# An attention + two-MoE kernel: the first duo transposed in two-token blocks, identity transposes ahead of it, and steps of the first expert's set-up moved

## The chip, the core and the metric

The kernel runs on one core of a Trainium2 chip. The metric is the device time of one execution, in microseconds. Before the change it was 596.75 us (median of three runs, 595.57 to 597.35).

## What is computed

Sigmoid attention, then two mixture-of-experts layers, all in fp32; `x` is the attention's output, a row per token with its 12 heads side by side.

```python
scores = scale * q @ k^T - log(S)            # 4 batches, 12 heads, S = 448, head_dim = 64
attn   = sigmoid(scores) @ v
# first MoE: rows with x @ w_skip > 0 only
e      = argmax(x @ w_gate)                  # 8 experts
y      = gate * (relu(x @ w1[e]) @ w2[e])    # 768 -> 1024 -> 768
x      = x + y
# second MoE: all rows
e      = argmax(normed(x) @ normed(emb)^T / tau)
out    = gate * (relu(x @ v1[e]) @ v2[e])
```

## The kernel before

The program is written out in order: each engine (PE is TensorE, ACT ScalarE, DVE VectorE, POOL GpSimd, SP the queue that issues most loads) works its own instructions strictly in that order and waits on semaphores.

**Attention** goes over 12 duos `w`, each four heads of a batch: `i` and `j` number the two pairs. A duo has 7 steps `h` of 64 keys. The loop counts `g = 7w + h`. In a step PE makes the scores of `h` (`score`, L596, four matmuls side by side into one of two `psS` tiles), ACT turns them into `A` by a sigmoid (L600), and two steps later PE multiplies `A` with `v` (`av`, L614) into two `psO` tiles. `take_x` (L523 on ACT, L525 on DVE) copies a finished duo's `psO` into `xT`. Loads of `k` and `q` of later duos are issued from SP (L553), of `v` from ACT (L565); from the second duo on, DVE transposes `k` and `q` in SBUF (`turn`, L587).

**The first duo** is loaded otherwise (L542): four consecutive tokens lie in one of 112 partitions, `(p c)` with `c` of 4. `turn_first` (L569) is called for k and q of `i = 0`, then of `i = 1`. For each `j` PE makes four transposes, one token of 64 values at a time (L575), and one copy takes the 64 x 448 result to `kT` or `qT`: DVE's for `j = 0` (L583), ACT's for `j = 1` (L581).

**Beside the attention** stand small steps, one list entry per `g`. When three batches are done (`b == B - 2`, at `g = 64`), a table `at` (L661) gives the steps for the first dense expert: `s1` to `s3` route batch 2; `gates` (L326) makes two sigmoids on ACT, then five DVE instructions; `plan_first` (L352) chooses a batch and expert on DVE; `start` reads the choice into registers and issues four weight loads of 768 KB on SP; `gate_cols` (L681) builds a diagonal matrix of the gates on DVE (L686); `rows` (L689) multiplies it with ones on PE (L692) and copies it back on ACT (L693); then seven calls of `split_gated` (L700), each a DVE product (L703), an ACT copy to the high part `xs` (L705) and a DVE subtraction for the low part (L706) of the chunk before.

**After the attention**, `split_unit` cuts weights into high and low parts (ACT L764, DVE L765) and `dense` (L774 to L776) makes three matmuls for each product.

Of the kernel before, what the change touches and what calls it, by code (L numbers as in the profile page):

```python
# [10 lines left out]
F32 = mybir.dt.float32  # L11
F32R = mybir.dt.float32r
I32 = mybir.dt.int32
AF = mybir.ActivationFunctionType
ALU = mybir.AluOpType
# [6 lines left out]
def sigmoid_attention_moe_moe_kernel(  # L22
# [15 lines left out]
    nc = tc.nc  # L38
# [287 lines left out]
    def gates(R, b0, b1):  # L326

        n = (b1 - b0) * C
        e = sm.tile([P, 2, (B - 1) * C, NE], F32, tag="ge", name="ge", bufs=1)
        s = sm.tile([P, B * C], F32, tag="gs", name="gs", bufs=1)  # L330
        sh = (R.SH[:, b0:b1] if R.m == 0 else R.SH).rearrange("p b c e -> p (b c) e")
        nc.scalar.activation(e[:, 0, :n], sh, AF.Sigmoid)
        nc.scalar.activation(e[:, 1, :n], sh, AF.Sigmoid, scale=-1.0)
        nc.vector.reciprocal(e[:, 1, :n], e[:, 1, :n])
        nc.vector.tensor_mul(e[:, 0, :n], e[:, 0, :n], e[:, 1, :n])
        nc.vector.reduce_sum(s[:, :n], e[:, 0, :n], axis=AX.X)
        nc.vector.tensor_single_scalar(s[:, :n], s[:, :n], 1e-9, op=ALU.add)
        nc.vector.reciprocal(K["gr"][R.m][:, b0:b1, :, 0], s[:, :n].rearrange("p (b c) -> p b c", c=C))

    def dense_gate(R, b, g=None):  # L340
        t = sm.tile([P, C, NE], F32, tag="dgt", name="dgt")
# [10 lines left out]
    def plan_first(R):  # L352

        n = B - 1
        t = sm.tile([128, 3, B], F32, tag="pl1", name="pl1", bufs=1)
        r = sm.tile([128, 4], F32, tag="pl1r", name="pl1r", bufs=1)
        fl = R.Fl[:, :n, 2]
        nc.vector.tensor_mul(t[:, 0, :n], fl, K["desc"][:, :n])
        nc.vector.reduce_max(r[:, 3:4], t[:, 0, :n], axis=AX.X)
        nc.vector.scalar_tensor_tensor(t[:, 1, :n], t[:, 0, :n], r[:, 3:4], fl, op0=ALU.is_equal, op1=ALU.mult)  # L360
        nc.vector.tensor_sub(K["rest"][:, :n], fl, t[:, 1, :n])
        nc.vector.tensor_single_scalar(r[:, 0:1], r[:, 3:4], 0.0, op=ALU.is_gt)
        nc.vector.tensor_mul(t[:, 2, :n], t[:, 1, :n], K["io"][:, :n])
        nc.vector.reduce_sum(r[:, 1:2], t[:, 2, :n], axis=AX.X)
        nc.vector.tensor_mul(t[:, 2, :n], t[:, 1, :n], R.Fl[:, :n, 3])
        nc.vector.reduce_sum(r[:, 2:3], t[:, 2, :n], axis=AX.X)
        nc.vector.tensor_copy(K["pa"][:, 0:3], r[:, 0:3])
# [159 lines left out]
    def attention():  # L527


        with ExitStack() as a:  # L530
# [27 lines left out]
            def load_v(w, *parts):  # L558
                b, d = duos[w]
                if "v" not in LDU[w]:  # L560
                    LDU[w]["v"] = ld.tile([128, 2, NH, D], F32, tag="v", name="v")
                t = LDU[w]["v"]
                for n in parts:
                    i, j = divmod(n, 2)
                    nc.scalar.dma_start(  # L565
                        t[KT * i : KT * i + KT, j], v[b, 4 * d + i + 2 * j].rearrange("(h r) d -> r h d", r=KT)
                    )

            def turn_first(nm, i):  # L569
                if i == 0:  # L570
                    ST[0, nm] = wk.tile([128, 2, S], F32, tag=nm + "T", name=nm + "T")
                ps = psS.tile([128, 2, 512], F32, tag="psS", name="ps_t")
                for j in range(2):
                    for c in range(C):
                        nc.tensor.transpose(  # L575
                            ps[:D, j, c * P : (c + 1) * P], LDU[0][nm][:, i, j, c * D : (c + 1) * D], ident[:P, :P]
                        )
                    src = ps[:D, j, :S].rearrange("r (c p) -> r p c", c=C)
                    dst = ST[0, nm][D * j : D * j + D, i].rearrange("r (p c) -> r p c", c=C)
                    if j:  # L580
                        nc.scalar.activation(dst, src, AF.Copy)  # L581
                    else:
                        nc.vector.tensor_copy(dst, src)  # L583

            def turn(w, nm):
                dst = ST[w, nm] = wk.tile([128, 2, S], F32, tag=nm + "T", name=nm + "T")
# [39 lines left out]
            nc.scalar.activation(bias, bias, AF.Sigmoid)  # L626
            nc.vector.memset(bias, -math.log(S))
            load_v(0, 0, 1, 2, 3)
            for i in range(2):
                turn_first("k", i)  # L630
                turn_first("q", i)
# [4 lines left out]
            for g in range(G + LAG):  # L636
                w, h = divmod(g, NH)
                if 0 < w < N - 2 and h == 0:
                    load_qk(w + 2)
                if g < G:  # L640
                    score(w, h)
                if w + 1 < N and 0 <= h - LAG < 4:
                    load_v(w + 1, h - LAG)
                if w + 1 < N and h in (3, 4):
                    turn(w + 1, "kq"[h - 3])
                for r in {LAG: (), LAG + 1: (LAG + 1, LAG)}.get(h, (LAG,)):
                    if g >= r:
                        av(*divmod(g - r, NH))
                for f in [todo.pop(0)] if todo and g >= 2 else late.get(g, ()):
                    if f:  # L650
                        f()
                done = g - LAG + 1
                if done % NH == 0 and done > 0:
                    b, d = duos[done // NH - 1]
                    if d == NP // 2 - 1 and b < B - 1:
                        assert not todo
                        s1, s2, s3 = route_stages(R1, b, x_of(b))
                        todo = [None, s1, s2, None, s3]
                        if b == B - 2:
                            fs = [s1, s2, s3, lambda: gates(R1, 0, B - 1), lambda: plan_first(R1)] + first_steps()  # L660
                            at = [g + i for i in (2, 3, 5, 8, 8, 10, 11, 12, 12, 13, 15, 16, 17, 18)] + [G]  # L661
                            todo, late = [], schedule({}, fs, at)
            return ST[N - 1, "o"]

# [45 lines left out]
    def first_steps():  # L710

        box = {}

        def start():
            pa = K["pa"]
            b = FIRST["b"] = nc.values_load(pa[0:1, 1:2], engines=XENG, min_val=0, max_val=B - 1)
            FIRST["e"] = nc.values_load(pa[0:1, 2:3], engines=[ENG.SP], min_val=0, max_val=NE - 1)
            load_unit(w1, w2, FIRST["e"], 0)
            load_unit(w1, w2, FIRST["e"], 1)
            box["p"] = split_gated(XST[0], b)  # L720

# [362 lines left out]
    def route2_steps(j, xs):  # L1084

        box = {}

        def halves(p):
            def f():
                if p == 0:  # L1090
                    box["b"] = batch_of(j)
                    box["p"] = split_batch(xs, box["b"])
                for g in box["p"][p : p + 2]:
                    g()

            return f

        return (
            [halves(p) for p in range(0, ND, 2)]
            + [lambda: raw(batch_of(j)), squares, squares_sum]  # L1100
            + route_stages(R2, j, lambda c: XR[:, c])
            + [scaled_logits, lambda: gates(R2, j, j + 1)]
        )


# [167 lines left out]
    nb_load = lambda: nc.values_load(K["pb"][0:1, 12:13], min_val=0, max_val=B - 1)  # L1273
    with tc.If(na > 0) as cmp:
        b, e = FIRST["b"], FIRST["e"]
        early = {0: s1, 2: s2, 4: s3, 5: [pl[0], lambda: gates(R1, B - 1, B)], 6: pl[1], 7: pl[2]}
        dense(XST[0], beside(units1(e), early), 0, NF // 2)
        NB["n"] = nb_load()
        with tc.If(NB["n"] > 0) as cmp2:
            steps = merge(next_dense(0), item_steps(R1, (10, 12, 15)), {12: lambda: raw(batch_of(0)), 15: squares})  # L1280
            dense(XST[0], beside(units1(e), steps), NF // 2)
            add_y(b)
            squares_sum()
            block1(1)
        with cmp2.Else():
            steps = merge(rest2(), item_steps(R1, (9, 11, 12)))
            dense(XST[0], beside(units1(e), steps), NF // 2)
            add_y(b)
            leftovers_now(lambda: start2(True))
            rare()  # L1290
    with cmp.Else():
        run({0: s1, 1: s2, 2: s3, 3: lambda: gates(R1, B - 1, B), 4: pl[0], 5: pl[1], 6: pl[2]})
        run(item_steps(R1, (0, 1, 2)))
        run(rest2())
        with tc.If(nb_load() > 0):
            run(next_dense(0))
            b, e = rest_regs(0)
            dense(XST[1], beside(units1(e), {}))
            add_y(b)
        leftovers_now(lambda: start2(True))  # L1300
        rare()
# [147 lines left out]
```

## Time and profile before

| | |
|---|---|
| median of the runs | 596.75 us |
| the profiled execution | 596.82 us |
| its span, first to last instruction | 595.0 us |
| PE busy | 572.8 us, 96% |
| DVE busy | 304.4 us, 51% |
| ACT busy | 275.2 us, 46% |
| fp32 score and value matmuls (L596, L614) | 88.2 and 86.4 us |

A line of the timeline gives start, duration, engine, line, operation, output and input tiles, the count of merged instructions, and in brackets the idle time before it and what ended that. `ACTq` and `SPq` are the issuing of DMAs by these engines. Each fp32 matmul of L596 and L614 is two records, each transpose one.

### The profile page before, as it was taken

The page shows a single profiled execution, that of the slowest core. Times are in us where ns is not written, and L with a number is a line of the kernel's source. Part 1 is how long each engine was busy: PE and PEld are TensorE (multiplying, and loading weights), DVE is VectorE, ACT ScalarE, POOL GpSimd, SP SyncE. Part 2 cuts the span into 40 slices and gives each one's busy share as a digit, 9 for nine tenths or more (in the row PEclk, how much of TensorE's full clock was granted, in tenths as well). Part 3 has the DMA queues.
Part 4 walks back from the last instruction along what each step waited for, and adds up shares of the span by engine and source line. Part 5 has one row for each costly group of instructions (what it writes and reads, how often), then busy time and mean ns, then how long its engine had stood idle before and what let it go on. Part 6 is the DMA issues. An engine that isn't in the chain of part 4 may idle for free. (4 is left out here: it accounts for less than half of the span.)

```text
span 595.0 us, 9925 instructions
## 1 busy us (share of the span) xinstructions
PE 572.8 (96%) x3722; PEld 440.0 (74%) x3722; DVE 304.4 (51%) x766; ACT 275.2 (46%) x447; POOL 7.5 (1%) x15
## 2 busy tenths in 40 slices
PE   5999999998999999999999999999999999999993
PEld 3365544534489897987868899979997999898881
DVE  2262435236757778562259664487347663542121
ACT  2676676666932374332138322752256322543020
POOL 2010000000000000000000000000000000000000
PEclk9999999999999999999999999999999999999997
DMA  9978877893460605234545060532317060642433
GB/s 150 117 118 132 109 120 109 122 119 87 166 204 6 209 4 165 103 107 159 188 158 190 2 211 1 188 118 80 133 58 248 1 214 0 223 159 83 159 108 100
DMA packets 139862, 73.31 MB, mean 123 GB/s; under 512 B 103858, under 2 KB 129798, under 8 KB 139792
## 3 DMA queue, kind: packets, MB, share of 16 engines
q1 hardware_dynamic: 116384, 65.94, 41.8%
q10 hardware_dynamic: 23216, 6.43, 6.0%
q8 instruction: 37, 0.61, 0.5%
q14 instruction: 33, 0.27, 0.1%
q0 software_dynamic: 192, 0.07, 0.1%
HBM read 66.90 MB, written 5.70 MB: 122 GB/s over the span
## 5 line engine op out<-in xcount | busy, mean ns | idle before, releaser
L774 PE MATMUL bank<-xs,h 128*128 128x448 f32 x288 | 107.6, 374 | 2.0 <-DVE xT L1165 0.9
L774 PE MATMUL y<-hh,h 128*128 128x448 f32 x288 | 108.5, 377 | 0.0
L794 ACT ACTIVATE hh<-bank 128x448 fp32r<-128x448 f32 x48 | 26.1, 543 | 177.4 <-PE bank L776 166.8
L775 PE MATMUL y<-hl,h 128*128 128x448 f32 x288 | 105.6, 367 | 0.0
L776 PE MATMUL y<-hh,l 128*128 128x448 f32 x288 | 105.6, 367 | 0.0
L776 PE MATMUL bank<-xs,l 128*128 128x448 f32 x288 | 105.3, 365 | 0.3 <-DVE l L765 0.3
L775 PE MATMUL bank<-xs,h 128*128 128x448 f32 x288 | 105.4, 366 | 0.0
L600 ACT ACTIVATE A<-psS,bias 128x896 f32<-128x896 f32 x84 | 83.4, 1006 | 35.9 <-PE psS L596 33.1
L596 PE MATMUL psS<-qT,kT 64*64 64x448 f32 x672 | 88.2, 554 | 0.0
L765 DVE TENSOR_TENSOR l<-r,h 128x512 fp32r<-128x512 f32 (+1 forms) x115 | 85.4, 792 | 4.8 <-ACT h L764 3.0
L795 DVE SCALAR_TENSOR_TENSOR hl<-bank,hh 128x448 fp32r<-128x448 f32 x48 | 29.9, 623 | 113.2 <-ACT hh L794 112.1
L614 PE MATMUL psO<-A,v 64*64 64x448 f32 x672 | 86.4, 539 | 0.0
L764 ACT ACTIVATE h<-r 128x512 fp32r<-128x512 f32 (+1 forms) x115 | 74.6, 710 | 0.0
L774 PEld LDWEIGHTS bank<-xs,h 128*128 128x128 f32 x288 | 54.0, 187 | 11.4 <-DVE hl L795 2.9
L774 PEld LDWEIGHTS y<-hh,h 128*128 128x128 f32 x288 | 54.1, 188 | 8.2 <-issue 2.9
L614 PEld LDWEIGHTS psO<-A,v 64*64 64x64 f32 x672 | 34.8, 133 | 32.3 <-issue 20.2
L776 PEld LDWEIGHTS bank<-xs,l 128*128 128x128 f32 x288 | 54.0, 188 | 5.5 <-DVE l L765 0.6
L776 PEld LDWEIGHTS y<-hh,l 128*128 128x128 f32 x288 | 54.1, 188 | 5.0
L775 PEld LDWEIGHTS y<-hl,h 128*128 128x128 f32 x288 | 54.2, 188 | 4.6 <-issue 0.2
L775 PEld LDWEIGHTS bank<-xs,h 128*128 128x128 f32 x288 | 54.1, 188 | 4.3
L596 PEld LDWEIGHTS psS<-qT,kT 64*64 64x64 f32 x672 | 32.8, 135 | 31.7 <-issue 17.4
L525 DVE COPY xT<-psO 64x448 f32<-64x448 f32 x24 | 14.9, 621 | 48.0 <-PE psO L614 47.7
(251 smaller groups left out, 452.8 us busy)
## 6 DMA issues: line engine op xcount, KB each, us to landing
r<-in_moe_w_dram SPq DMA_DIRECT2D x62, 768.0 KB, 5.9
v<-in_v_dram ACTq DMA_DIRECT2D x48, 112.0 KB, 3.6
k<-in_k_dram SPq DMA_DIRECT2D x44, 112.0 KB, 3.6
q<-in_q_dram SPq DMA_DIRECT2D x44, 112.0 KB, 4.0
out_dram<-row SPq DMA_DIRECT2D x3, 1344.0 KB, 6.9
out_dram<-row SPq DMA_DIRECT2D x1, 896.0 KB, 5.5
stg<-in_moe_w_dram SPq DMA_DIRECT2D x1, 768.0 KB, 6.4
row<-in_moe_w_dram SPq DMA_DIRECT2D x1, 768.0 KB, 8.2
```

Of the source, the lines that this page charges most:

```text
L525: nc.vector.tensor_copy(x, ps[64 * j : 64 * j + 64, :S])
L596: nc.tensor.matmul(ps[KT * i : KT * i + KT, j, :S], lhsT=kT[r, i, h * KT : (h + 1) * KT], rhs=qT[r, i], start=True, stop=True,)
L600: nc.scalar.activation(at, ps[:, :, :S], AF.Sigmoid, bias=bias, scale=1.0 / math.sqrt(D))
L614: nc.tensor.matmul(ST[w, "o"][i][D * j : D * j + D, :S], lhsT=t[r, j, h, :], rhs=at[r, j, :], start=h == 0, stop=h == NH - 1,)
L764: nc.scalar.activation(dst_h, src, AF.Copy)
L765: nc.vector.tensor_sub(dst_l, src, dst_h.bitcast(F32))
L774: nc.tensor.matmul(ps, lhsT=ah, rhs=bh, start=first, stop=False)
L775: nc.tensor.matmul(ps, lhsT=ah, rhs=bl, start=False, stop=False)
L776: nc.tensor.matmul(ps, lhsT=al, rhs=bh, start=False, stop=last)
L794: nc.scalar.activation(a, ps[:, :S], AF.Relu)
L795: nc.vector.scalar_tensor_tensor(l, ps[:, :S], 0.0, a.bitcast(F32), op0=ALU.max, op1=ALU.subtract)
```

## The change

`turn_first` now transposes two tokens (128 values) at a time, so a call makes four transposes of 112 x 128 instead of eight of 112 x 64, all into one `psA` bank. A token's 64 values lie in one half of the result's partitions, so each `j` needs two copies of 64 x 224 that write every second column: two on DVE, then two on ACT. Ahead of the calls PE makes 14 transposes of the identity into a `psO` tile that nobody reads. `gates` is cut into its ACT part and a function with its DVE part; the ACT part moves from step 8 to 5 of the table, the DVE part to 7, `gate_cols` from 11 to 10, and the calls of `split_gated` but the last one step back each. Elsewhere `gates` is called as a whole, as before.

```diff
+        def rest():
+            nc.vector.reciprocal(e[:, 1, :n], e[:, 1, :n])
...
+        return rest
@@ turn_first
-                ps = psS.tile([128, 2, 512], F32, tag="psS", name="ps_t")
+                ps = bank("ps_t")
                 for j in range(2):
-                    for c in range(C):
+                    for e in range(2):
                         nc.tensor.transpose(
-                            ps[:D, j, c * P : (c + 1) * P], LDU[0][nm][:, i, j, c * D : (c + 1) * D], ident[:P, :P]
+                            ps[:, (2 * j + e) * P : (2 * j + e + 1) * P],
+                            LDU[0][nm][:, i, j, 2 * e * D : (2 * e + 2) * D], ident[:P, :P],
                         )
-                    src = ps[:D, j, :S].rearrange("r (c p) -> r p c", c=C)
-                    dst = ST[0, nm][D * j : D * j + D, i].rearrange("r (p c) -> r p c", c=C)
-                    if j:
-                        nc.scalar.activation(dst, src, AF.Copy)
-                    else:
-                        nc.vector.tensor_copy(dst, src)
+                for j in range(2):
+                    for o in range(2):
+                        src = ps[D * o : D * o + D, 2 * j * P : (2 * j + 2) * P].rearrange("r (e p) -> r p e", e=2)
+                        dst = ST[0, nm][D * j : D * j + D, i].rearrange("r (p e o) -> r p e o", e=2, o=2)[:, :, :, o]
+                        if j:
+                            nc.scalar.activation(dst, src, AF.Copy)
+                        else:
+                            nc.vector.tensor_copy(dst, src)
@@ attention
+            busy = psO.tile([128, 512], F32, tag="psO", name="busy")
+            for _ in range(14):
+                nc.tensor.transpose(busy[:, :128], ident, ident)
...
-                            at = [g + i for i in (2, 3, 5, 8, 8, 10, 11, 12, 12, 13, 15, 16, 17, 18)] + [G]
+                            at = [g + i for i in (2, 3, 5, 5, 7, 8, 10, 10, 12, 13, 15, 16, 17, 18, 19)] + [G]
```

PE at the program's start (`ps_t` holds a call's transposes, `psS` the first scores); before:

```order
L1444 UNCONDITIONAL_BRANCH
L575 MATMUL ps_t_141<-ident_81,k0_127 64x112 x8
L575 MATMUL ps_t_153<-ident_81,q0_128 64x112 x8
L575 MATMUL ps_t_164<-ident_81,k0_127 64x112 x8
L575 MATMUL ps_t_175<-ident_81,q0_128 64x112 x8
L596 MATMUL psS_207<-qT_152,kT_140 64x448 x4
```

and now:

```order
L1457 UNCONDITIONAL_BRANCH
L638 MATMUL busy_140<-ident_81 128x128 x14
L579 MATMUL ps_t_156<-ident_81,k0_127 128x112 x4
L579 MATMUL ps_t_166<-ident_81,q0_128 128x112 x4
L579 MATMUL ps_t_175<-ident_81,k0_127 128x112 x4
L579 MATMUL ps_t_184<-ident_81,q0_128 128x112 x4
L603 MATMUL psS_214<-qT_165,kT_155 64x448 x4
```

Sixteen transposes stand where 32 did, behind 14 new ones.

ACT at the same place, with the semaphores that its instructions wait for (`DMAHW` is a load's, `DVE` and `PE` are those engines'); before:

```order
L565 DMA v<-in_v_dram 64x7x64 [waits DMAHW0_49]
L565 DMA v<-in_v_dram 64x7x64 [waits DMAHW2_49]
L581 ACTIVATE kT<-ps_t 64x448 [waits DVE_49,PE_49]
L581 ACTIVATE qT<-ps_t 64x448 [waits DVE_49,PE_49]
L581 ACTIVATE kT<-ps_t 64x448 [waits DVE_49,PE_49]
L581 ACTIVATE qT<-ps_t 64x448 [waits DVE_49,PE_49]
L600 ACTIVATE A<-psS,bias 128x896 [waits PE_49] x3
```

and now:

```order
L569 DMA v<-in_v_dram 64x7x64 [waits DMAHW0_49]
L569 DMA v<-in_v_dram 64x7x64 [waits DMAHW2_49]
L588 ACTIVATE kT<-ps_t 64x224 [waits DVE_49,PE_49]
L588 ACTIVATE kT<-ps_t 64x224
L588 ACTIVATE qT<-ps_t 64x224 [waits DVE_49,PE_49]
L588 ACTIVATE qT<-ps_t 64x224
L588 ACTIVATE kT<-ps_t 64x224 [waits DVE_49,PE_49]
L588 ACTIVATE kT<-ps_t 64x224
L588 ACTIVATE qT<-ps_t 64x224 [waits DVE_49,PE_49]
L588 ACTIVATE qT<-ps_t 64x224
L607 ACTIVATE A<-psS,bias 128x896 [waits PE_49] x3
```

Two half copies stand for each copy; the first of each pair waits for DVE's pair of the same call, as the whole copy did for DVE's.

ACT at the gates (`ge`) and at the end of the attention (`xs` is `split_gated`'s copy, `h` the first weight split); before, from the sigmoid of step 81 on:

```order
L600 ACTIVATE A_1637<-psS_1638,bias_86 128x896
L705 ACTIVATE xs0_93<-xg1_74 128x448
L600 ACTIVATE A_1651<-psS_1652,bias_86 128x896
L705 ACTIVATE xs0_93<-xg0_73 128x448
L600 ACTIVATE A_1665<-psS_1666,bias_86 128x896
L705 ACTIVATE xs0_93<-xg1_74 128x448
L764 ACTIVATE h10_1704<-r10_89 128x512 x3
```

and now:

```order
L607 ACTIVATE A_1641<-psS_1642,bias_86 128x896
L718 ACTIVATE xs0_93<-xg0_73 128x448
L607 ACTIVATE A_1655<-psS_1656,bias_86 128x896
L718 ACTIVATE xs0_93<-xg1_74 128x448
L607 ACTIVATE A_1669<-psS_1670,bias_86 128x896
L718 ACTIVATE xs0_93<-xg0_73 128x448
L718 ACTIVATE xs0_93<-xg1_74 128x448
L777 ACTIVATE h10_1711<-r10_89 128x512 x3
```

Two `xs` copies instead of one now stand between the last sigmoid and the first weight split. On DVE the gates, the plan, the two transposes and the diagonal follow each other in the same order as before.

## Rows read from the trace of the kernel before

**Rows 1.** The page: busy time of each engine and its share.

```profile
PE 572.8 (96%) x3722; PEld 440.0 (74%) x3722; DVE 304.4 (51%) x766; ACT 275.2 (46%) x447; POOL 7.5 (1%) x15
```

**Rows 2.** Stretches: bounds, length, PE busy (records), granted clock, DMA share, GB/s.

```profile
20.10:144.40 124.30, 124.30 (x1254) 1.00 0.76 112
144.40:146.40 2.00, 0.00 (x0) 1.00 0.51 94
159.70:585.60 425.90, 422.44 (x2282) 1.00 0.37 124
```

**Rows 3.** Timeline, PE, 4 to 20 us.

```profile
4.49 0.92 PE L575 MATMUL ps_t<-ident,k 112*64 112x112 f32 x4 [4.49 <-DMA k<-in_k_dram]
6.12 0.96 PE L575 MATMUL ps_t<-ident,k 112*64 112x112 f32 x4 [0.71 <-DVE kT L583]
6.87 0.95 PE L575 MATMUL ps_t<-ident,q 112*64 112x112 f32 x4
...
14.24 6.02 PE L596 MATMUL psS<-qT,kT 64*64 64x448 f32 x32
```

**Rows 4.** Timeline, ACT and DVE, 4 to 18 us.

```profile
4.75 2.29 ACTq L565 DMA_DIRECT2D v<-in_v_dram  x2
5.45 0.62 DVE L583 COPY kT<-ps_t 64x448 f32<-64x448 f32 x1 [2.12 <-PE ps_t L575]
...
7.15 0.54 ACT L581 ACTIVATE kT<-ps_t 64x448 f32<-64x448 f32 x1 [3.94 <-PE ps_t L575]
...
14.35 0.54 ACT L581 ACTIVATE qT<-ps_t 64x448 f32<-64x448 f32 x1 [1.87 <-PE ps_t L575]
...
16.73 1.01 ACT L600 ACTIVATE A<-psS,bias 128x896 f32<-128x896 f32 x1 [1.84 <-PE psS L596]
17.22 1.11 DVE L587 STREAM_TRANSPOSE qT<-q 128x896 f32<-128x896 f32 x1 [1.98 <-DMA q<-in_q_dram]
```

**Rows 5.** Timeline, short instructions that follow each other on ACT and DVE.

```profile
139.04 0.27 ACT L332 ACTIVATE ge<-SH 112x96 f32<-112x96 f32 x1
139.22 0.27 ACT L333 ACTIVATE ge<-SH 112x96 f32<-112x96 f32 x1
...
145.56 0.84 DVE L686 TENSOR_SCALAR G<-ident,dg 112x112 f32<-112x112 f32 x4
```

**Rows 6.** Timeline, PE, scores and values later; POOL, the identity's last instruction.

```profile
1.01 0.29 POOL masks.py:199 TENSOR_SCALAR_AFFINE_SELECT ident<-ident 128x128 f32<-128x128 f32 x1
...
20.09 1.68 PE L614 MATMUL psO<-A,v 64*64 64x448 f32 x16
21.59 0.93 PE L596 MATMUL psS<-qT,kT 64*64 64x448 f32 x8
```

**Rows 7.** Timeline, PE, transposes near the end of the span.

```profile
578.66 0.38 PE L1326 MATMUL y<-ident,stg 128*112 128x128 f32 x2
578.88 0.38 PE L1326 MATMUL bank<-ident,stg 128*112 128x128 f32 x2
```

**Rows 8.** Timeline, DVE and PE around the gates and the diagonal.

```profile
136.65 1.26 DVE L525 COPY xT<-psO 64x448 f32<-64x448 f32 x2 [0.54 <-PE psO L614]
139.52 0.75 DVE L334 RECIPROCAL ge<-ge 112x96 f32<-112x96 f32 x1 [1.61 <-ACT ge L333]
...
146.45 1.02 PE L692 MATMUL ps_G<-G,one 112*128 112x448 f32 x2 [2.06 <-DVE G L686]
```

**Rows 9.** Timeline, ACT, DVE and PE where the attention ends.

```profile
157.62 1.01 ACT L600 ACTIVATE A<-psS,bias 128x896 f32<-128x896 f32 x1
...
158.53 0.57 ACT L705 ACTIVATE xs<-xg 128x448 fp32r<-128x448 f32 x1
...
159.13 0.62 DVE L706 TENSOR_TENSOR xs<-xg,xs 128x448 fp32r<-128x448 f32 x1 [0.74 <-ACT xs L705]
159.87 1.89 DVE L765 TENSOR_TENSOR l<-r,h 128x512 fp32r<-128x512 f32 x3
160.62 0.47 PE L776 MATMUL bank<-xs,l 128*128 128x448 f32 x1 [0.27 <-DVE l L765]
```

More of the change, by code (lines that the diff above doesn't have):

```diff
@@ L333, in gates @@
         nc.scalar.activation(e[:, 1, :n], sh, AF.Sigmoid, scale=-1.0)
[L334 to L338, printed above, removed]
+        def rest():
+            nc.vector.reciprocal(e[:, 1, :n], e[:, 1, :n])
+            nc.vector.tensor_mul(e[:, 0, :n], e[:, 0, :n], e[:, 1, :n])
+            nc.vector.reduce_sum(s[:, :n], e[:, 0, :n], axis=AX.X)
+            nc.vector.tensor_single_scalar(s[:, :n], s[:, :n], 1e-9, op=ALU.add)
+            nc.vector.reciprocal(K["gr"][R.m][:, b0:b1, :, 0], s[:, :n].rearrange("p (b c) -> p b c", c=C))
+        return rest
     def dense_gate(R, b, g=None):
@@ L659, in attention @@
                         if b == B - 2:
-                            fs = [s1, s2, s3, lambda: gates(R1, 0, B - 1), lambda: plan_first(R1)] + first_steps()
-                            at = [g + i for i in (2, 3, 5, 8, 8, 10, 11, 12, 12, 13, 15, 16, 17, 18)] + [G]
+                            ge = []
+                            fs = [
+                                s1, s2, s3, lambda: ge.append(gates(R1, 0, B - 1)), lambda: ge[0](), lambda: plan_first(R1),
+                            ] + first_steps()
+                            at = [g + i for i in (2, 3, 5, 5, 7, 8, 10, 10, 12, 13, 15, 16, 17, 18, 19)] + [G]
                             todo, late = [], schedule({}, fs, at)
@@ L1101, in route2_steps @@
             + route_stages(R2, j, lambda c: XR[:, c])
-            + [scaled_logits, lambda: gates(R2, j, j + 1)]
+            + [scaled_logits, lambda: gates(R2, j, j + 1)()]
         )
@@ L1275, in sigmoid_attention_moe_moe_kernel @@
         b, e = FIRST["b"], FIRST["e"]
-        early = {0: s1, 2: s2, 4: s3, 5: [pl[0], lambda: gates(R1, B - 1, B)], 6: pl[1], 7: pl[2]}
+        early = {0: s1, 2: s2, 4: s3, 5: [pl[0], lambda: gates(R1, B - 1, B)()], 6: pl[1], 7: pl[2]}
         dense(XST[0], beside(units1(e), early), 0, NF // 2)
@@ L1291, in sigmoid_attention_moe_moe_kernel @@
     with cmp.Else():
-        run({0: s1, 1: s2, 2: s3, 3: lambda: gates(R1, B - 1, B), 4: pl[0], 5: pl[1], 6: pl[2]})
+        run({0: s1, 1: s2, 2: s3, 3: lambda: gates(R1, B - 1, B)(), 4: pl[0], 5: pl[1], 6: pl[2]})
         run(item_steps(R1, (0, 1, 2)))
```

## Prediction

> **What bounds the kernel now.** I read the page's busy times first: PE is busy for 572.8 us, 96%, no other engine for more than 51% [rows 1]. The table by stretches says where PE is not busy: nowhere from 20.1 to 144.4 us, for all of the 2.0 us that follow, and for 3.5 of the 425.9 us of dense work [rows 2]. So what comes sooner ahead of these stretches comes sooner at the end, one for one, as long as nothing else becomes late. The change touches three places: the opening, where scores start only at 14.24 us [rows 3], the hole of 2 us, and the passage from attention to dense work. I went through the timelines of these three.
>
> The granted clock stands at 1.00 in every stretch [rows 2], yet the work of the opening is slower than that. Four transposes of 112 columns took 0.75 us from start to start (6.12 to 6.87), 1.67 ns a column [rows 3]; near the end two of 128 columns take 0.22 us, 0.85 ns a column [rows 7]. That is the lower level of the clock, 1.2 GHz, against 2.4. It lasts into the scores: their first 32 records take 14.24 to 20.09 us, 5.85, and the 16 records that follow 1.50 [rows 3, 6].
>
> **The opening.** A call of `turn_first` now is: four transposes (0.75), DVE's copy (0.62), four transposes that wait for it, ACT's copy (0.54) [rows 3, 4]. Four calls fill 4.49 to 14.24; the last copy ends at 14.35 + 0.54 = 14.89, and the scores of `j = 1` follow it at about 14.94.
>
> In the new order a call is four transposes, DVE's pair of half copies, ACT's pair, and two banks alternate. The prices: a whole copy is 0.62 on DVE and 0.54 on ACT. Splitting adds one start. ACT takes 0.54 for 448 columns and 1.01 for 896, 1.05 ns a column [rows 4]; its two sigmoids of 96 columns start 0.18 apart [rows 5], of which 0.10 are columns, so a start is 0.08. DVE's four instructions of 112 columns take 0.21 each [rows 5], 0.12 of it columns, so 0.09. I take 0.65 for ACT's pair and 0.70 for DVE's, near these rows. Below stands the whole copy alone (0.54 and 0.62, the start hidden). Above I put two whole copies (1.08 and 1.24), because no row shows a copy that writes every second column.
>
> The chain on the trace's clock:
> - ACT is not free before 4.75 + 2.29 = 7.04, when it has issued the last loads of `v` [rows 4]. By then PE and DVE have done with k and q of `i = 0` (4.49 + 1.5 + 0.2, then 0.70).
> - ACT: k 7.10 to 7.75, q to 8.40.
> - PE gets the first bank back at 7.80: transposes of k (`i = 1`) end at 8.75, with 0.20 for the last one to come out (5.45 less 4.49 less 0.75), of q at 9.50.
> - DVE: k 8.79 to 9.49, q 9.54 to 10.24. ACT: k 9.53 to 10.18, q, after DVE's pair, 10.28 to 10.93.
> - The scores of `j = 1` start at 10.98 instead of 14.94: **3.96 us sooner**. With the low prices it is 4.26, with the high ones 2.07.
>
> The 14 identity transposes cost nothing if they fit before k lands. The identity is ready at 1.30 [rows 6]; 14 of 128 columns at 1.67 ns are 3.0 us, to about 4.4, and k's first transpose starts at 4.49. If each took twice as long, its weight load unhidden, they would end at 7.3, k's copies on ACT would begin near 9.2 instead of 7.10, and 2.1 of the 3.96 would be lost.
>
> What is late next: the second duo's q. DVE waits for its load until 17.22 and ends at 18.33 [rows 4]. It is needed by the eighth score, which comes after the first two value products and three more steps, each 1.50 [rows 6]: 20.09 + 4 x 1.50 = 26.1. 3.96 sooner this is 22.1, so 3.8 us are left and no new wait arises.
>
> **The clock.** My sum leaves the clock as it was: low for most of the first four scores. In the trace 32 transposes between 4.49 and 14.24, with waits of 0.71 us among them, had not raised it when the scores began [rows 3]. The Trainium skill ("TensorE: Matmul & The Clock Gate", Part 4) says that transposes do not count as activity of TensorE in the way matmuls do, and that full clock does not engage for them. By that rule the 14 transposes change no time and the sum stays as it is, 591.9; the trace agrees as far as it goes. That they do raise the clock, 590.2, is the first rival.
>
> **Gates, plan and diagonal.** PE reaches the product with the diagonal at 144.40 and waits 2.06 us for DVE [rows 8]. DVE's work before it has no hole from the reciprocal at 139.52 to the end of the diagonal at 145.56 + 0.84 = 146.40 [rows 5, 8], 6.88 us, and the new order keeps it. But the reciprocal itself waited 1.61 us for ACT's sigmoids, which came at 139.04 and 139.22 behind another sigmoid. They now come three steps earlier, about 4.5 us, long before DVE needs them. DVE then starts when `take_x` is done, 136.65 + 1.26 = 137.91, and ends near 144.83. PE waits 0.48 instead of 2.06: **1.57 us gained**. The rest of the wait is DVE's own work. Moving `gate_cols` one step forward changes nothing by itself, since nothing stands between it and its predecessor on DVE.
>
> **The passage to dense work.** Before, one `xs` copy stood between the last sigmoid and the first weight split on ACT (158.53, then 158.99), and its subtraction ended on DVE at 159.75, just when the last value products did; the low part of the weights started at 159.87 and PE's first use of it at 160.62 [rows 9]. Now two copies and two subtractions stand there. The first subtraction takes the place of the one before, the second adds 0.62, so the low part starts 0.6 later: **0.58 us lost**. Below it is nothing, if the steps before leave DVE ahead; above 1.2, a copy and a subtraction in full (0.57 + 0.62). In between the number of copies from one sigmoid to the next is unchanged.
>
> **Sum.** 3.96 + 1.57 - 0.58 = 4.95. The profiled execution took 596.82 us, of which 595.0 are span; it lies 0.07 above the median, so nothing is corrected. 596.82 - 4.95 = **591.9 us**.
>
> **Rivals.**
> - *The clock rises before the scores.* For it: the new transposes fill the whole array and PE works without a break from 1.3 to some 6 us, which it did nowhere in the opening before. Against it: the 32 transposes above. Price: the last two calls' transposes at half, one of which is on the path, 0.37; and the first four scores. From the start t of the `j = 1` scores the first sigmoid then comes at t + 1.05 (1.79 before, less 0.75 of matmul), sigmoids of 1.01 follow each other, the fourth score waits for the second of them and ends at t + 3.85, where it was 20.09 - 14.94 = 5.15. That is 1.3, with the 0.37 together 1.7: 590.2 us.
> - *Half copies at the price of whole ones*, or identity transposes that hold up k: 2.07 instead of 3.96, so 593.8 us. For it: the column step has no row. Against it: the whole copy already reads PSUM in a permuted order at the price of a plain one, 0.62.
> - *The hole stays*, since DVE's chain is held by something that ACT's wait hid (the loads for the two DVE transposes in it): the 1.57 are not gained, 593.4 us. Against it: 2.0 us of the chain would have to be late by chance in the same amount.
> - *Slower than before*: the pairs of half copies are four in the chain after 7.1 (ACT k, ACT q, DVE q, ACT q, with 0.95 of transposes), so it reaches 14.94 plus the 1.0 of the other places when a pair costs 1.97 us; at 2.5 us it is 3.1 later and the time 599 us. For it there is no row, only the lack of one; against it the columns' price, a third of that.
>
> **How the numbers follow.** My forecast gets 0.52, the early clock 0.26, the dear copies 0.12, the hole 0.06, the slower case 0.04. The likeliest is 591.9. The range leaves out the slower case and the edges: 589.3 (the early clock with the low copy prices and 0.6 for the passage not lost) to 594.0 (the dear copies). A measurement of this kernel tells about 0.3%, 1.8 us, from no change, so the first three cases and the hole are faster; the dear copies with a full loss in the passage, or the hole with half of them, end within it. Faster 0.90, same 0.06, slower 0.04.
>
> **What would show it.** The first scores at 10.3 to 10.5 and the first sigmoid at 12.8 instead of 16.73; pairs of half copies of 0.65 and 0.70; the fourth score's end a little over 5 us after the scores' start (low clock) or under 4 (early clock); PE's wait for the diagonal at 0.5; DVE's reciprocal of the gates right behind `take_x`; PE's first use of low weights about 0.6 later against the last value product. It is wrong if ACT is not the engine that paces the opening from 7.1 on, if k's first transposes start after 4.6, or if PE waits anew between the second duo's first score and 144 us.

## The result, and the profile after

The changed kernel takes 591.5 us, the median of four runs (590.88 to 592.26), where the kernel before took 596.88 beside it: ratio 0.9914, 95% interval 0.9892 to 0.9936. The forecast was 591.9, range 589.3 to 594.0. The profiled execution took 592.26 us, 590.5 of them span; the one before 596.82 and 595.0. So 4.56 us went, where the sum said 4.95. A second set of runs gave 590.74 against 596.37, ratio 0.9907 [0.9892, 0.9923].

PE's busy time hardly changed (the page; before: [rows 1]). On balance, what went is time in which PE waited, 22.2 us of the span before (595.0 less 572.8) and 17.1 now (590.5 less 573.4):

```profile
PE 573.4 (97%) x3720; PEld 437.7 (74%) x3720; DVE 304.9 (52%) x770; ACT 276.3 (47%) x451; POOL 7.5 (1%) x15
```

The opening in the timeline of the changed kernel (start, duration, and the rest as in [rows 3]), for [rows 3, 4, 6]. L579 are the transposes, L590 DVE's half copies, L588 ACT's, L603 the scores, L607 the sigmoids, L621 the value products, L638 the identity transposes, L569 the loads of `v`:

```profile
1.35 3.25 PE L638 MATMUL busy<-ident 128*128 128x128 f32 x14 [1.35 <-POOL ident masks.py:199]
...
4.43 1.01 PE L579 MATMUL ps_t<-ident,k 112*128 112x112 f32 x4
4.80 2.69 ACTq L569 DMA_DIRECT2D v<-in_v_dram  x2
5.23 0.64 PE L579 MATMUL ps_t<-ident,q 112*128 112x112 f32 x4
...
7.60 0.73 ACT L588 ACTIVATE kT<-ps_t 64x224 f32<-64x224 f32 x2 [4.39 <-DVE qT L590]
8.36 0.74 ACT L588 ACTIVATE qT<-ps_t 64x224 f32<-64x224 f32 x2
8.39 0.64 PE L579 MATMUL ps_t<-ident,k 112*128 112x112 f32 x4 [2.52 <-ACT kT L588]
...
9.15 1.01 PE L579 MATMUL ps_t<-ident,q 112*128 112x112 f32 x4
...
10.09 7.11 PE L603 MATMUL psS<-qT,kT 64*64 64x448 f32 x32
...
11.08 0.74 ACT L588 ACTIVATE qT<-ps_t 64x224 f32<-64x224 f32 x2 [0.40 <-DVE qT L590]
13.66 1.01 ACT L607 ACTIVATE A<-psS,bias 128x896 f32<-128x896 f32 x1 [1.84 <-PE psS L603]
...
17.02 1.31 PE L621 MATMUL psO<-A,v 64*64 64x448 f32 x12
```

The first value products start at 17.02 us instead of 20.09: 3.07 are gained. PE waits 2.52 us, from the end of q's transposes on, for the bank that ACT gives back, and ACT starts at 7.60, right after its second load of `v` is issued (4.80 + 2.69 = 7.49). The first sigmoid comes 1.84 us after ACT's last copy, as before [rows 4]: the scores ran at the same low clock.

But that clock had been high in between. The table by stretches (bounds, length, PE busy with its records, granted clock, DMA share, GB/s):

```profile
6.00:8.30 2.30, 0.00 (x0) 1.00 1.51 131
8.30:10.00 1.70, 1.48 (x8) 0.65 1.51 100
10.00:12.00 2.00, 2.00 (x9) 0.50 1.43 146
```

The transposes show the same. k's first four follow each other at 0.20 us on average (5.23 less 4.43, by four); the q group takes 0.64 us to the end of its last instead of 1.01; k's second group takes 0.64, q's second 1.01 again. So PE came to 2.4 GHz during q's first transposes, having done transposes only; it then stood idle until 8.39, and the clock fell back to 1.2 GHz at 8.82, within the second calls and ahead of the scores. It rose for good only at 15.65 us. (The 1.00 of the first stretch is no sign of a high clock by itself: the view of before gives 1.00 for 4.4 to 14.2 us too, where the transposes are slow.)

The gates and the passage (timeline; before: [rows 8, 9]):

```profile
133.91 1.26 DVE L529 COPY xT<-psO 64x448 f32<-64x448 f32 x2 [0.54 <-PE psO L621]
135.09 0.74 DVE L336 RECIPROCAL ge<-ge 112x96 f32<-112x96 f32 x1
...
142.00 1.02 PE L705 MATMUL ps_G<-G,one 112*128 112x448 f32 x2 [0.34 <-DVE G L699]
...
154.06 1.14 ACT L718 ACTIVATE xs<-xg 128x448 fp32r<-128x448 f32 x2
...
155.11 1.66 ACT L777 ACTIVATE h<-r 128x512 fp32r<-128x512 f32 x3
...
155.77 0.47 PE L787 MATMUL bank<-xs,h 128*128 128x448 f32 x1 [0.49 <-ACT h L777]
...
156.51 0.47 PE L789 MATMUL bank<-xs,l 128*128 128x448 f32 x1
```

The reciprocal stands right behind `take_x` without a wait, and PE waits 0.34 us for the diagonal instead of 2.06: by the start of this product 4.45 us are gained (146.45 less 142.00). At the first use of the low weights it is 4.11 (160.62 less 156.51): the passage lost 0.34, and PE's wait has moved from the low part to the high part of the weights. Two places were not in the sum. From 37 us on 0.33 us were lost, where ACT idles 1.48 us ahead of a sigmoid instead of 1.14; the same loss stands in all six profiles that have this opening with `v` on ACT and gaps unfilled, with or without identity transposes, and in no other. And 0.53 came back near 225 us, where PE's wait for `xT` shrank; the second line is of a second profile of the same kernel:

```profile
220.41 0.45 PE L787 MATMUL bank<-xs,h 128*128 128x448 f32 x1 [0.33 <-DVE xT L1178]
220.20 0.44 PE L787 MATMUL bank<-xs,h 128*128 128x448 f32 x1 [0.86 <-DVE xT L1178]
```

It was 0.86 at 225.04 in the kernel before too, so the 0.53 is chance and not the change: over all profiles here this wait is 0.21 to 0.86.

### The profile page after: what moved, and what is told of

Same layout as the page of the kernel before. It is cut to its first block, busy times and chain, and to the rows that moved or that the text cites. A ratio compares the mean times of both kernels' runs of the same rounds, so it can differ in the third digit from the quotient of the medians.

```text
span 590.5 us, 9926 instructions
## 1 busy us (share of the span) xinstructions
PE 573.4 (97%) x3720; PEld 437.7 (74%) x3720; DVE 304.9 (52%) x770; ACT 276.3 (47%) x451; POOL 7.5 (1%) x15
## 5 line engine op out<-in xcount | busy, mean ns | idle before, releaser
L607 ACT ACTIVATE A<-psS,bias 128x896 f32<-128x896 f32 x84 | 83.5, 1007 | 36.3 <-PE psS L603 35.9
L603 PE MATMUL psS<-qT,kT 64*64 64x448 f32 x672 | 90.5, 554 | 0.0
L621 PE MATMUL psO<-A,v 64*64 64x448 f32 x672 | 87.3, 538 | 0.0
L621 PEld LDWEIGHTS psO<-A,v 64*64 64x64 f32 x672 | 34.0, 133 | 33.7 <-issue 22.8
L603 PEld LDWEIGHTS psS<-qT,kT 64*64 64x64 f32 x672 | 32.2, 135 | 34.2 <-issue 20.0
```

The costliest lines, as they stand in the source:

```text
L603: nc.tensor.matmul(ps[KT * i : KT * i + KT, j, :S], lhsT=kT[r, i, h * KT : (h + 1) * KT], rhs=qT[r, i], start=True, stop=True,)
L607: nc.scalar.activation(at, ps[:, :, :S], AF.Sigmoid, bias=bias, scale=1.0 / math.sqrt(D))
L621: nc.tensor.matmul(ST[w, "o"][i][D * j : D * j + D, :S], lhsT=t[r, j, h, :], rhs=at[r, j, :], start=h == 0, stop=h == NH - 1,)
```

## The experiments

Each is named by what it changes. "Values" is the start of the first value products in its profile. A ratio is to runs of the kernel before on the same chip.

| kernel | median us | ratio to before [interval] | values at |
|---|---|---|---|
| before | 596.0 to 596.9 | | 20.09 |
| the table alone | 594.08 | 0.9960 [0.9944, 0.9976] | 19.64 |
| changed | 591.5; 590.74 | 0.9914 [0.9892, 0.9936]; 0.9907 [0.9892, 0.9923] | 17.02; 16.25 |
| changed, no identity transposes | 589.3; 589.27 | 0.9889 [0.9871, 0.9907]; 0.9883 [0.9862, 0.9904] | 16.17; 17.12 |
| changed, gaps filled | 588.45 | 0.9869 [0.9848, 0.9891] | 15.03 |
| changed, v's last loads on SP | 588.76 | 0.9874 [0.9854, 0.9894] | 14.67 |
| the last, no identity transposes | 588.03 | 0.9862 [0.9840, 0.9884] | 15.29 |
| v on SP and gaps filled | 588.22 | 0.9867 [0.9849, 0.9885] | 14.46 |
| and copies by operand | 588.31 | 0.9862 [0.9843, 0.9880] | 14.32 |
| changed, chunks back | 590.36 | 0.9900 [0.9878, 0.9923] | 16.87 |
| changed, no column step | 592.03 (one run) | | 17.04 |
| all that helped | 587.41 | 0.9852 [0.9828, 0.9875] | 13.68 |

**The table alone**: the kernel before, with the cut `gates` and the new list `at`.

> The kernel before with the new table of steps and the cut gates alone; first duo transposed as before, no identity transposes. Theory: PE's wait for the diagonal goes from 2.06 to about 0.4 us and the passage to dense work gives 0.35 back, so 1.3 to 1.4 us less than the kernel before: 595.5 us. Rival (the hole is filled but the time comes back in dense work): 596.5 to 597 us.

It took 594.08 us, 2.3 less than before. In its trace the diagonal's product gains 1.71 us against the kernel before and the passage loses 0.35, the amounts of the changed kernel (1.71 and 0.34); 0.44 more had come in the opening, 0.08 of it because k landed sooner and the rest with the clock's rise at 17.26 instead of 18.96 us, and 0.63 came at the varying wait for `xT` (0.23 at 222.58). So it is neither the theory's 1.3 to 1.4 nor the rival's: the amount forecast came, and what is above it is not the table's. The two halves of the change are thus independent at the diagonal and the passage.

**Gaps filled**: 16 and 12 more identity transposes, so that PE does not stand idle while it waits for ACT.

```diff
             for i in range(2):
                 turn_first("k", i)
                 turn_first("q", i)
+                for _ in range((16, 12)[i]):
+                    nc.tensor.transpose(busy[:, :128], ident, ident)
```

> The changed kernel with 16 more identity transposes after the calls for i = 0 and 12 after those for i = 1, so that TensorE does not stand idle between 5.9 and 8.4 us nor before the scores. Theory (transposes raise the clock and hold it as long as they follow each other): the first scores run at the higher level, the fourth score ends under 4.3 us after the j = 1 scores start instead of 5.15, 590.0 us. Rival (the page's rule, transposes don't engage the clock; the rise at 5.41 was chance): first scores at the lower level, 591.5 to 592.5 us, or later if the added transposes hold up k of i = 1.

588.45 us. The clock rose once, at 5.51 us, and stayed (stretches; timeline; L643 are the added transposes):

```profile
6.00:8.30 2.30, 1.82 (x18) 1.00 1.53 128
...
10.00:12.00 2.00, 2.00 (x22) 1.00 1.43 141
```

```profile
5.73 1.91 PE L643 MATMUL busy<-ident 128*128 128x128 f32 x16
...
8.12 0.60 PE L579 MATMUL ps_t<-ident,k 112*128 112x112 f32 x4 [0.48 <-ACT kT L588]
8.89 0.60 PE L579 MATMUL ps_t<-ident,q 112*128 112x112 f32 x4 [0.16 <-ACT qT L588]
...
12.27 1.91 ACT L607 ACTIVATE A<-psS,bias 128x896 f32<-128x896 f32 x2 [1.05 <-PE psS L603]
```

Until 10.7 us PE had done nothing but transposes. They raised the clock and held it while they followed each other with waits of 0.48 us at most; the idle time is what let it fall in the changed kernel. From ACT's last copy to the first sigmoid it is 1.05 us instead of 1.84. From the scores of `j = 1`, whose single records start at 11.26 and in the changed kernel at 11.87, it is 1.01 to the first sigmoid (the prediction's early clock had 1.05) and 3.77 instead of 5.15 to the value products: 1.4 us, near the rival's 1.3. The total gains more than the theory's 590.0, but 1.3 to 1.5 us of it lie behind PE's last matmul (8.07 us to the span's end instead of 9.4 to 9.5) and are not the clock's; more on that below.

**v's last loads on SP**: of `v`'s four loads the last two, which ACT issued at 4.80 to 7.49 us, go to SP's queue.

```diff
-            load_v(0, 0, 1, 2, 3)
+            load_v(0, 0, 1)
+            load_v(0, 2, 3, queue=nc.sync)
```

> The changed kernel with the last two of the first duo's four v loads issued from SP instead of ACT, so that ACT need not wait for q's landing before its first copy. Theory (ACT's start at 7.60 paces the opening): ACT's first pair starts at 6.3, the scores of j = 1 about 1.2 us earlier, at 10.6 to 10.8, 590.3 us. Rival (the loads themselves pace it, or the second duo's loads come later): 591.5 us or more, with a new wait of PE or DVE for a load.

588.76 us, less than the theory's 590.3. ACT is free at 5.45 and works from 6.20, as soon as DVE has its pair (timeline):

```profile
4.85 0.60 ACTq L569 DMA_DIRECT2D v<-in_v_dram  x1
...
6.20 0.73 ACT L588 ACTIVATE kT<-ps_t 64x224 f32<-64x224 f32 x2 [2.98 <-DVE kT L590]
...
9.34 0.74 ACT L588 ACTIVATE qT<-ps_t 64x224 f32<-64x224 f32 x2
11.91 1.91 ACT L607 ACTIVATE A<-psS,bias 128x896 f32<-128x896 f32 x2 [1.83 <-PE psS L603]
```

ACT's last copy ends 1.74 us sooner than in the changed kernel (9.34 against 11.08, equal lengths), the value products come 2.35 sooner. Of the 1.74, 1.40 is ACT's sooner start (6.20 against 7.60) and 0.34 lies in the second calls, where q's transposes ran at the high clock (0.60 us instead of 1.01). The other 0.61 is again the clock, which fell here too (1.83 from copy to sigmoid) but came back at 11.7 us. That ACT's issue paced the opening from 7.1 us on is shown: taken away, the opening moved.

**No identity transposes**, run twice.

```diff
-            busy = psO.tile([128, 512], F32, tag="psO", name="busy")
-            for _ in range(14):
-                nc.tensor.transpose(busy[:, :128], ident, ident)
```

> The changed kernel without the 14 identity transposes. Theory (they carry little: in the changed kernel's trace the clock rises to its higher level at 5.41 us but falls again at 8.82, before the scores): 591.3 to 592.2 us, against 596.9 for the kernel before and 591.5 for the changed one; the scores of j = 1 start at 11.9 and run at the lower level. Rival (the identity transposes carry part of the gain through the clock): 592.5 us or more.

> The changed kernel without the 14 identity transposes, a second time. Theory (as the change stands they buy nothing and can cost: with them the clock rises early and falls again before the scores; the four profiles with them show value products at 16.25 to 17.04 us, the one without at 16.17): value products at 16.0 to 16.4 again, clock rising once, between 12.5 and 14 us, ratio 0.987 to 0.989. Rival (the single profile without them met a lucky moment of the rise): rise near 15 us, value products near 17, ratio 0.990 to 0.992 as with them.

589.3 and 589.27 us, less than the changed kernel's 591.5 and 590.74 and than both the first run's theory and its rival; the intervals of the ratios overlap. The two profiles contradict each other on the opening (values at 16.17, then 17.12; the clock rose at 13.48, then 15.11), and so do those of the changed kernel (17.02, then 16.25), so the 14 transposes, as the change places them, buy nothing there that these profiles can show. The rival of the second run, a lucky moment, holds for the first profile, though the ratio came as the theory had it. PE's last matmul ends at 579.57 and 580.77 us without them and at 580.94 and 580.43 with them, so most of the gain is not in the opening. Against the table alone (19.64) the new order of transposes and copies, without identity transposes, brings the value products 2.5 to 3.5 us sooner, so it carries the gain of the opening by itself. What is steady lies elsewhere, behind PE's last matmul. The DMA view of the last 20 us (queue, size, us from issue to landing) of the changed kernel:

```profile
out_dram<-row ACTq DMA_DIRECT2D x1, 448.0 KB, 6.4
out_dram<-xg,small POOLq DMA_INDIRECT x1, 3.5
```

and of the second run without them:

```profile
out_dram<-row ACTq DMA_DIRECT2D x1, 448.0 KB, 5.2
out_dram<-xg,small POOLq DMA_INDIRECT x1, 2.3
```

Both stores land about 1.2 us sooner, one behind the other, and from PE's last matmul to the span's end it is 6.9 to 7.0 us instead of 9.4 to 9.5. That the transposes are missing, 570 us earlier, is not enough for it: the kernel before and the table alone have none of them and take 9.4 and 9.3. The trace holds one difference that goes with it. The DMA view of the 5 us behind PE's last matmul has, for the queue that it calls `instruction` (packets, MB, share), in the changed kernel, the first run without the transposes and the kernel with filled gaps:

```profile
q8 instruction: 3, 0.05, 5.7%
q8 instruction: 1, 0.02, 1.8%
q8 instruction: 2, 0.03, 2.5%
```

It is 3 packets of 16 KB in all ten profiles with the long end (8.8 to 9.5 us), 1 in the three without identity transposes, whose previous packet had started before PE's last matmul ended, and 2 with filled gaps, where only the second store lands sooner. So more loads of the program's own instructions fall among the last stores in some builds than in others. That they are the cause was not tested.

**v on SP, no identity transposes.**

> The last two v loads on SP, without the identity transposes. Theory (the transposes buy clock time in the opening, and ACT no longer paces it): the clock stays at 1.2 GHz from the start until within the scores; transposes of 1.0 instead of 0.6 us a call put j=1 scores near 10.5 instead of 10.1; value products at 15.0 to 15.6 instead of 14.7: 0.3 to 0.9 us more than with v on SP and the transposes, 589.0 to 589.7. Rival (they buy nothing, since the clock falls again before the scores; it rises sooner for a steady load without that fall): value products at 14.7 or sooner, 588.8 or less.

588.03 us, with the same short landings (5.3 and 2.3 us, against 6.3 and 3.2 with v on SP and the transposes). The time alone would speak for the rival, but it is the end's: PE's last matmul ends at 579.00 us, 0.74 later than with the transposes. The profile leans to the theory as far as the opening goes:

```profile
4.82 0.98 PE L579 MATMUL ps_t<-ident,k 112*128 112x112 f32 x4 [4.82 <-POOL io_i L100]
...
7.51 1.01 PE L579 MATMUL ps_t<-ident,k 112*128 112x112 f32 x4 [0.96 <-ACT kT L588]
...
15.29 1.68 PE L621 MATMUL psO<-A,v 64*64 64x448 f32 x16
```

The transposes stay at 1.0 us a group, and values come 0.62 later than with the 14 transposes (15.29 against 14.67). Of this 0.33 is k's own start (4.82 against 4.49), which follows k's landing and was 4.40 to 5.24 over all profiles. The 0.29 that are left are less than two profiles of one kernel differ by (0.77 and 0.95), so what the transposes are worth here is not shown.

**The changed kernel again**, unaltered.

> The changed kernel once more, unaltered, beside the others of this group. Theory (the opening is set by waits, the clock's moments by what PE did just before): 590.9 to 592.3 us, ratio 0.990 to 0.993; in the profile the clock is at 2.4 GHz over the first transposes of q and falls to 1.2 GHz before the scores, value products start at 16.9 to 17.1 us. Rival (the moments of the clock are an accident of the single profile): the scores of the opening run at the other level, value products start near 15.7 us or near 18.3.

590.74 us, 0.2 under the theory's range; its ratio, 0.9907, came and its profile did not. The clock rose at 6.34 us, at the end of q's first transposes (0.95 us, still slow), fell at 9.75, and came back at 13.17 instead of 15.65, and values at 16.25 instead of 17.02. How long the clock stays low is not set by the kernel alone; it is worth 0.8 us between two profiles of the same kernel.

**Half copies without the column step.**

```diff
-                        dst = ST[0, nm][D * j : D * j + D, i].rearrange("r (p e o) -> r p e o", e=2, o=2)[:, :, :, o]
+                        dst = ST[0, nm][D * j : D * j + D, i, 2 * o * P : (2 * o + 2) * P].rearrange("r (p e) -> r p e", e=2)
```

> The changed kernel, but each half copy writes 224 columns side by side instead of every second one (so k's and q's columns of the first duo stand in another order). Theory (the column step makes the pairs longer than forecast): ACT's pairs 0.65 us instead of 0.73, DVE's 0.70 instead of 0.79, j=1 scores about 0.25 us sooner. Rival (two starts and 448 columns cost this in any order): pairs stay at 0.73 and 0.79 and the opening is as it was.

One run, 592.03 us. The pairs (timeline):

```profile
6.44 0.79 DVE L590 COPY qT<-ps_t 64x224 f32<-64x224 f32 x2
...
7.69 0.71 ACT L588 ACTIVATE kT<-ps_t 64x224 f32<-64x224 f32 x2 [4.48 <-DVE qT L590]
```

DVE's stay at 0.79, ACT's lose 0.02 of the 0.73. The column step costs almost nothing; the rival holds. What I had priced too low is the start. In the changed kernel one half copy takes 0.36 us on ACT and 0.39 on DVE (columns: line, shape and count | busy, mean ns of one | idle before):

```profile
L590 DVE COPY qT<-ps_t 64x224 f32<-64x224 f32 x4 | 1.6, 388 | 0.4 <-PE ps_t L579 0.3
L588 ACT ACTIVATE kT<-ps_t 64x224 f32<-64x224 f32 x4 | 1.4, 361 | 5.3 <-DVE qT L590 4.4 <-DVE kT L590 0.8
```

**v on SP and gaps filled**, with 10 and 8 transposes, since the gaps are shorter.

> The last two v loads on SP and, in one kernel, identity transposes in the two gaps of the opening (10 and 8). Theory (the two gains are separate: ACT's free time and the clock): j=1 scores at 10.1 us as with v on SP alone, but at 2.4 GHz, so the first sigmoid at 11.1 instead of 11.9 and value products at 13.9 instead of 14.7: 0.8 us less than with v on SP alone, about 588.0 us. Rival 1 (they gain the same time only once): 588.8. Rival 2 (the transposes after the second call hold up the j=0 scores): scores start at 8.8 but j=1 not later, no loss; if j=1 comes at 10.9, 588.8 to 589.5.

588.22 us, no less than either alone within the intervals. In this profile k's transposes began at 5.24 instead of 4.49 with v on SP alone, which hid the gain: from the start of k's transposes to the value products it is 9.22 us (14.46 less 5.24) against 10.18 (14.67 less 4.49), 0.96 less, where the theory had 0.8.

**Copies by operand**: as the last kernel, with k's four half copies on DVE and q's on ACT.

```diff
-                        if j:
+                        if nm == "q":
```

> As the kernel with v on SP and filled gaps, and each call's four half copies on one engine: k's on DVE, q's on ACT, so that no ACT pair waits for a DVE pair of the same bank. Theory: DVE has k of i=0 from 5.3 to 6.9, ACT q from 5.5 to 7.0; the second calls' transposes start at 6.9 and 7.0, DVE's four from 7.5 to 9.1, ACT's from 7.8 to 9.3; all scores from 9.35 us instead of j=1 at 10.1; first sigmoid near 10.7, value products near 13.5: 587.6 us. Rival (the path is DVE's or ACT's sum of copies either way): first sigmoid at 11.1 or later, 588.0 us or more.

588.31 us, the same as without it: the rival's numbers. The first sigmoid came at 11.56, not 10.7. In this profile the clock rose only at 6.79 us, so q's first transposes took 0.95 and ACT began at 6.39; the theory's times were for the sooner rise, which the run with all parts had.

**Chunks back**: the calls of `split_gated` where they were before, the rest of the table as changed.

```diff
-                            at = [g + i for i in (2, 3, 5, 5, 7, 8, 10, 10, 12, 13, 15, 16, 17, 18, 19)] + [G]
+                            at = [g + i for i in (2, 3, 5, 5, 7, 8, 10, 10, 12, 12, 13, 15, 16, 17, 18)] + [G]
```

> The changed kernel with the calls of split_gated where they were before (first at step 12, one xs copy left after the last sigmoid); gates, plan and diagonal stay moved. Theory (the second copy and subtraction ahead of the weight split cost the passage 0.35 us): PE waits for the diagonal 0.34 us as in the changed kernel; one xs copy between the last sigmoid and the weight split; PE's wait of 0.49 for the first high weights goes and the first low weights come 0.35 us sooner against the last value product; 0.3 to 0.4 us less than the changed kernel, about 590.4 on its 590.7. Rival (the loss has another place, such as take_x or the weights' landing): the passage stays as it is, no gain.

590.36 us, which can't be told from 590.74. The passage (timeline):

```profile
141.84 1.02 PE L705 MATMUL ps_G<-G,one 112*128 112x448 f32 x2 [0.35 <-DVE G L699]
...
153.91 0.57 ACT L718 ACTIVATE xs<-xg 128x448 fp32r<-128x448 f32 x1
154.38 1.66 ACT L777 ACTIVATE h<-r 128x512 fp32r<-128x512 f32 x3
...
155.06 0.47 PE L787 MATMUL bank<-xs,h 128*128 128x448 f32 x1
...
156.00 0.47 PE L789 MATMUL bank<-xs,l 128*128 128x448 f32 x1 [0.27 <-DVE l L778]
```

From the diagonal's product to the first low weights it is 14.16 us (156.00 less 141.84) instead of 14.51 in the changed kernel: the 0.35 is back, PE's wait for the high weights gone, the wait for the diagonal unchanged. So the second chunk ahead of the weight split is the cause.

**All that helped**: v's loads on SP, gaps filled with 10 and 8, copies by operand, chunks back.

> All that helped: v's last two loads on SP, gaps filled with 10 and 8 identity transposes, k's copies on DVE and q's on ACT, split_gated's calls where they were before. Theory (gains in different places add): value products at 14.3 us when k lands as in the kernel with copies by operand, the passage 0.35 us shorter: 0.3 to 0.4 less than that kernel, about 587.9, ratio 0.985 to 0.986. Rival (an earlier start of the scores only moves a wait to the second duo's k or to the hole): PE waits anew for k's transpose near 20 us or for the diagonal, 588.3 or more.

587.41 us, ratio 0.9852 [0.9828, 0.9875], the lowest median here, though its interval overlaps those of the others with `v` on SP. Its opening has the sooner clock (4.77 us), and scores, first sigmoid and value products lie within 0.25 us of the times that the theory gave for copies by operand (timeline):

```profile
5.29 1.60 DVE L590 COPY kT<-ps_t 64x224 f32<-64x224 f32 x4 [1.95 <-PE ps_t L579]
...
5.74 1.52 ACT L588 ACTIVATE qT<-ps_t 64x224 f32<-64x224 f32 x4 [2.52 <-PE ps_t L579]
...
9.11 2.53 PE L603 MATMUL psS<-qT,kT 64*64 64x448 f32 x16
10.92 1.91 ACT L607 ACTIVATE A<-psS,bias 128x896 f32<-128x896 f32 x2 [1.05 <-PE psS L603]
...
13.68 1.68 PE L621 MATMUL psO<-A,v 64*64 64x448 f32 x16
```

Its opening is 0.64 us ahead of the same opening in the kernel with copies by operand (13.68 against 14.32), by the moment of the clock alone as far as the two profiles show. Its last stores have the long landing (6.3 and 2.9 us).

## Why the prediction was right, step by step

The time was right to 0.4 us, and each of the three places moved as said; one size was off in the opening, and one reason was not sound. That it came so close has luck in it: the three places gave 4.44 us in the profile (3.07 + 1.71 - 0.34) and not 4.95, what was outside the sum nearly cancels, and the opening alone moves by 0.8 us between two profiles of the changed kernel.

- *The opening, 3.96 forecast, 3.07 measured.* The pacer was right: ACT's issue of `v`, then ACT's pairs. `j = 1` scores came at 11.87 instead of 10.98, and so the first sigmoid at 13.66 instead of 12.8. Of the 0.89, 0.50 is ACT's start (7.60 instead of 7.10, its second load waits for q to land, which varies by run), and the other 0.39 nearly all the pairs: four of them lie on the path from 7.60 to 11.82, at 0.73 to 0.79 instead of 0.65 and 0.70. The mis-sized term is the start of a copy. I read it off instructions of 96 and 112 columns that follow each other [rows 5], which start closer together than half copies do: two ACT half copies stand 0.37 apart, 0.24 of it columns at 1.05 ns, so a start is 0.14, not 0.08. The rival of dear copies (2.07 gained) was too dark, and the column step, of which no row had told, costs next to nothing (0.01 us a half copy on ACT). In the second profile `j = 1` scores start at the same time, 11.86, and 3.84 are gained, by the clock.
- *The clock, "left as it was".* The number held in the first profile: from the `j = 1` scores to the value products it is 5.15 us before and after. That was luck, for in the second profile it is 4.39. The reason did not hold. The rule of the Trainium skill that I had set beside it ("TensorE: Matmul & The Clock Gate", Part 4), that full clock does not engage for transposes, disagrees with these traces: the clock rose in the changed kernel at 5.41 us and in the one with filled gaps at 5.51 us, with transposes only. The trace of before seems to have agreed with the rule by its waits of 0.71 us among the transposes and not by their kind: the new transposes, too, left the clock low until 12.04 to 15.11 us in the three profiles in which they stand among waits with no identity transposes ahead. The rival of the early clock saw the rise and missed the fall behind the 2.5 us in which PE waits for ACT; with the gaps filled its price (1.3) was right.
- *The identity transposes cost nothing.* This held: by their modelled ends they last to 4.6 us, yet k's first transposes start at 4.43, as soon as k has landed (4.39) and under the 4.6 that I had set. (The second profile has 4.62, because k landed at 4.57; without identity transposes k starts as late, at 4.57, 4.73 and 4.82.) That they also bring anything in this place is not shown.
- *The second duo's q, 3.8 us of slack.* It was transposed from 17.43 to 18.54 and nothing waited for it.
- *Gates and diagonal, 1.57 forecast, 1.71 measured.* Both signs came: the reciprocal right behind `take_x`, and the wait at 0.34 (0.48 forecast). The table alone gave the same 1.71.
- *The passage, 0.58 lost forecast, 0.34 measured.* The place and the cause were right, as the run with the chunks put back shows. The loss is smaller, since PE had waited 0.27 for the low part before and now waits for the high part instead; the low weights follow the high ones without a new wait. The 0.53 that the first profile wins back near 225 us is no part of it: the second profile waits 0.86 there, as before.
- *The balance.* 3.07 - 0.33 + 1.71 - 0.34 + 0.53 is 4.64, and the span lost 4.57. The end of the program, 9.37 us after PE's last matmul before and 9.52 now, took 0.15 of it; other waits gave 0.1 back.

Two things stay open: the 0.33 us near 37 us, a small case of the new delay before 144 us that I had named as a sign of being wrong, and whether the instruction loads are what makes the last stores land sooner in the three runs without the identity transposes. I did not run the fastest version without its 14 first transposes, which would have shown whether the short end adds to its gain.

## What to carry to other kernels

Where a chain of small copies sets the time, price a split copy by its start as well as its columns, from an instruction of about that size; and look for what the copying engine issues ahead of its first copy, since moving two loads to another queue let the first copy start 1.4 us sooner. Dummy work that is to raise PE's clock should last until the real work begins: 14 transposes ahead of a wait of 2.5 us gave nothing that shows, filling the wait brought the value products 1.2 to 2.0 us sooner. Compare openings by the trace, not by the total: a difference of 2.4 us at the end of the program, far from the edit's work, was larger than the effect that was looked for. And take a second profile of the same kernel before a small gain is put down to the change: the 0.53 us near 225 us went away with it.

## What the runs showed of the hardware

- Transposes alone, one behind the other, brought PE from 1.2 to 2.4 GHz (at 4.07 to 6.79 us over the profiles of kernels that begin with 14 of them), and where the gaps were not filled PE fell back at 7.49 to 9.75 us, before or within the second calls, after waits of 1.33 to 2.85 us; with gaps filled (waits of 0.63 us at most) it did not, in four profiles. The moment of rise and fall varied from run to run of one kernel, by up to 2.5 us for the last rise, and with it the opening by 0.8 us.
- A copy of 64 x 224 from PSUM took 0.36 us on ACT and 0.39 on DVE, whether it wrote every column or every second one (0.35 and 0.39).
- The landing of the last two stores, the same in every kernel, took 6.3 to 6.4 and 2.9 to 3.5 us in ten profiles, 5.2 to 5.3 and 2.3 in the three without identity transposes that have the new order, and 6.4 and 2.3 in the one with filled gaps; between the two extremes lie up to 2.6 us of the span. With it goes the count of 16 KB instruction packets in the 5 us behind PE's last matmul: 3, 1 and 2.
